# Down product of four experts: tokens moving in rows of 512, output stored by feature

## The chip, the cores and the metric

One core of one Trainium2 chip. The metric is the device time of one execution in microseconds, here the median of three runs. The core's engines are TensorE (PE in the profile; PEld is its weight load), VectorE (DVE), ScalarE (ACT), GpSimd (POOL) and SyncE (SP), whose queue issues most DMAs. SBUF is the working memory, PSUM the eight banks that TensorE writes; a bank holds 512 fp32 numbers in each of 128 partitions.

## The reference

Three layers in a row on B = 2 batches of S = 768 tokens, 1,536 tokens in all, with 384 features each.

```python
# 1: linear attention with decay, 8 heads of 48
for t in range(S):
    state = alpha[:, :, t, :, None] * state + einsum('bhd,bhe->bhde', k[:, :, t], v[:, :, t])
    y[:, :, t] = einsum('bhd,bhde->bhe', q[:, :, t], state)
# 2: RMS norm and a gated layer, 384 -> 1536 -> 384
xn = x / sqrt(mean(x * x, -1) + 1e-6) * rms_g
g = xn @ w_gate
x = (g * sigmoid(g) * (xn @ w_val)) @ w_out
# 3: four experts, 384 -> 1024 -> 384, each token with its own shares
p = domain_probs / (domain_probs.sum(-1, keepdims=True) + 1e-9)
for e in range(4):
    h = maximum(x @ w1[e], 0.0)
    out += p[:, e:e + 1] * (h @ w2[e])
```

The change touches the last line, the product with w2 and its weighting by the shares.

## The kernel before

Every fp32 product is made of three products in a reduced fp32 format: each operand is split into a high and a low part (whi and wlo, hh and hl), and high x low, high x high and low x high are added up in one PSUM bank. This is `mm3`, lines 907 to 911, so all dense matmuls bear the lines L909, L910 and L911. The three matmuls differ in the stationary operand (lhsT, loaded by a weight load) and in the moving one, whose columns stream through.

The tokens are worked in three blocks of 512. Attention goes chunk by chunk (128 tokens) and is mixed into the first two blocks of the gated layer. All work is recorded in a plan, whose list scheduler gives each operation a planned start from planned costs, due paths and buffers; the operations are then issued in that order, each on its engine's queue. There are two plans. The first holds attention and the gated layer for blocks 0 and 1, with some 35 matmuls on zeros (`idle`, L1070) that fill planned gaps of TensorE at the start. The second holds block 2 of the gated layer and the experts.

In the gated layer's down step (`outs` in `block1`) the weights are stationary and 512 hidden tokens move; its output stands by feature, three banks of 128 features. In the trace these are the rows `o<-hl,whi`, `o<-hh,whi`, `o<-hh,wlo`, 128x512. The stretch called the dense block below is block 2 of this layer and the part of block 1 without attention, from some 230 to 300 us.

The expert stage has 96 steps: expert e, block blk, and eight pieces f of 128 hidden features. An up step (`e_up`) is nine 512-wide matmuls (x2 moving) into a bank g or ph, then ScalarE's Relu (hh, L1252) and VectorE's remainder (hl, L1257). A down step (`e_down`) takes hh and hl as stationary operands, 128 tokens at a time, and moves 384 columns of w2: four token tiles of three matmuls, rows `o<-wlo,hh`, `o<-whi,hh`, `o<-whi,hl` and the same with pe. Each tile has its own bank for the eight pieces, three o banks and one pe bank. Behind the eighth piece VectorE multiplies each tile by the token's share, a scalar per partition (`pr`), and adds it to `acc` (L1291 for expert 0, L1297 after), and for the last expert SP stores the tile (L1306), 128 tokens of 384 features. On TensorE the order is up step n, then down step n - 1; only at the start stand three up steps and then two down steps.

At the end a flag decides whether `general`, a slow fallback without the splitting, runs; in this profile it doesn't.

Of the kernel before, what the change touches and what calls it, by code (L numbers as in the profile page):

```python
# [19 lines left out]
P = 128  # L20
# [208 lines left out]
def general(tc, const, af, kq, v, w64, w32, out):  # L229
# [6 lines left out]
    with ExitStack() as ctx:  # L236
# [137 lines left out]
        for e in range(E):  # L374
# [4 lines left out]
            for blk in range(4):  # L379
# [11 lines left out]
                for t in range(3):  # L391
# [16 lines left out]
                    if e == E - 1:  # L408
                        r0 = blk // 2 * S + (blk % 2 * 3 + t) * C
                        nc.sync.dma_start(out=out[r0 : r0 + C, :], in_=acc[i])  # L410
# [3 lines left out]
def body(ctx: ExitStack, tc: tile.TileContext, af, kq, v, w64, w32, rms_g, probs, out):  # L414
# [31 lines left out]
    x2_dram = dram.tile([P, KD, 512], F32, name="x2_dram")  # L446

# [609 lines left out]
    def idle(start, end):  # L1057

        gap = end - start - 0.2 - (COLD if start < 2 else 0)
        many = lambda a: a.unsqueeze(1).to_broadcast([P, 4, P])  # L1060
        row = floor[:, :512].bitcast(F32R)
        kinds = (
            (zw, zeros), (zw, row), (zw, ones[:, :1].bitcast(F32R).to_broadcast([P, 512])),
            (zw, many(zw)), (zw[:, :64], row),
            (zw.bitcast(BF16)[:, :P], floor[:, :256].bitcast(BF16)),
        )
        for n in range(max(0, round(gap / 0.22)) if start else 0):
            w, x = kinds[nfill[0] // 4 % len(kinds)]
            to = first[0]()[: w.shape[1]]
            nc.tensor.matmul(to, lhsT=w, rhs=x, start=False, stop=False)  # L1070
            nfill[0] += 1

    nfill = [0]
# [93 lines left out]
    for n in block1([(1, slice(0, 512), f) for f in range(12)]):  # L1167
# [5 lines left out]
        if n == 10:  # L1173
            plan.op("DVE", 0.5, norm_probs, r=[("x2_dram", 0)], w=["pr"])

# [89 lines left out]
    pe = {}  # L1265

    def e_down(e, blk, f):
        key = (19 + 4 * e + 2 * (f // 4), f // 2 % 2)
        hh, hl = hq.pop((e, blk, f))
        if f == 0:  # L1270
            for t in range(4):
                pe[t] = obank() if t < 3 else plan.tile(psl, [P, 512], F32, "pe", 1)
        for t in range(4):
            i = 4 * blk + t
            p, a = pe[t], acc[i]

            def go(t=t, p=p):
# [9 lines left out]
            p1 = pr[:, i, e : e + 1]  # L1287
# [99 lines left out]
```

## Time and profile before

| | us |
|---|---|
| median of 3 runs (lowest, highest) | 711.68 (711.62, 712.18) |
| the profiled execution's own time | 711.74 |
| its span, first to last instruction | 710.0 |
| TensorE busy | 697.9 |
| VectorE busy | 310.7 |
| ScalarE busy | 198.7 |

Matmuls are pipelined: a printed length of 0.39 us for a 512-wide one overlaps its neighbours, so the spacing of starts is what a matmul costs. A group's row gives count, busy time and mean length; a timeline row gives start, length, engine, line and tiles, and in brackets the idle time before it with what ended it.

### The profile page before, as it was taken

The page shows a single profiled execution, that of the slowest core. Times are in us where ns is not written, and L with a number is a line of the kernel's source. Part 1 is how long each engine was busy: PE and PEld are TensorE (multiplying, and loading weights), DVE is VectorE, ACT ScalarE, POOL GpSimd, SP SyncE. Part 2 cuts the span into 40 slices and gives each one's busy share as a digit, 9 for nine tenths or more (in the row PEclk, how much of TensorE's full clock was granted, in tenths as well). Part 3 has the DMA queues.
Part 4 walks back from the last instruction along what each step waited for, and adds up shares of the span by engine and source line. Part 5 has one row for each costly group of instructions (what it writes and reads, how often), then busy time and mean ns, then how long its engine had stood idle before and what let it go on. Part 6 is the DMA issues. An engine that isn't in the chain of part 4 may idle for free.

```text
span 710.0 us, 9804 instructions
## 1 busy us (share of the span) xinstructions
PE 697.9 (98%) x4164; PEld 610.4 (86%) x4164; DVE 310.7 (44%) x522; ACT 198.7 (28%) x406; POOL 12.9 (2%) x26
## 2 busy tenths in 40 slices
PE   8989999999999999999999999999999999999996
PEld 6889887778888888789999999999899999999996
DVE  7899999993223544432223512133312121222212
ACT  3754544543222433421113311123111111111110
POOL 1010000000000000000000000000000000000000
PEclk9999999999999999999999999999999999999999
DMA  9843554250000241310001310001000000001001
GB/s 263 262 135 109 170 192 140 78 195 2 0 1 1 90 133 46 134 45 1 1 1 44 92 42 0 1 1 44 1 1 1 0 1 1 0 1 45 23 22 47
DMA packets 13873, 42.02 MB, mean 59 GB/s; under 512 B 1856, under 2 KB 4928, under 8 KB 13824
## 3 DMA queue, kind: packets, MB, share of 16 engines
q1 hardware_dynamic: 13536, 41.32, 18.1%
q8 instruction: 33, 0.54, 0.3%
q14 instruction: 16, 0.13, 0.1%
q10 hardware_dynamic: 288, 0.03, 0.0%
HBM read 38.19 MB, written 3.15 MB: 58 GB/s over the span
## 4 chain that ended last, share of the span: by engine, by line
PE 81%; DVE 13%; DMA 3%; issue 1%; SPq 1%; ACT 0%; DVEq 0%; ACTq 0%
PE o L909 10%; PE o L911 10%; PE o L910 10%; PE g L909 9%; PE g L910 9%; PE g L911 9%; PE ph L910 5%; PE ph L911 5%; PE ph L909 5%; DMA raw<-in_w 3%; PE pe L910 2%; PE pe L909 2%; PE pe L911 2%; DVE cv L582 2%; DVE cv L574 2%; DVE wlo L517 1%
## 5 line engine op out<-in xcount | busy, mean ns | idle before, releaser
L909 PE MATMUL g<-x1l,whi 128*128 128x512 f32 (+1 forms) x384 | 146.5, 382 | 0.0
L911 PE MATMUL g<-x1h,wlo 128*128 128x512 f32 (+1 forms) x384 | 145.3, 378 | 0.0
L910 PE MATMUL g<-x1h,whi 128*128 128x512 f32 (+1 forms) x384 | 145.3, 378 | 0.0
L911 PE MATMUL o<-whi,hl 128*128 128x384 f32 x288 | 97.5, 339 | 0.0
L909 PE MATMUL o<-wlo,hh 128*128 128x384 f32 x288 | 97.3, 338 | 0.0
L910 PE MATMUL o<-whi,hh 128*128 128x384 f32 x288 | 96.9, 337 | 0.0
L1257 DVE SCALAR_TENSOR_TENSOR hl<-ph,hh 128x512 fp32r<-128x512 f32 x48 | 33.2, 691 | 128.3 <-ACT hh L1252 128.3
L1257 DVE SCALAR_TENSOR_TENSOR hl<-g,hh 128x512 fp32r<-128x512 f32 x48 | 33.0, 688 | 119.0 <-ACT hh L1252 119.0
L911 PEld LDWEIGHTS g<-x1h,wlo 128*128 128x128 f32 x384 | 72.2, 188 | 13.4
L909 PEld LDWEIGHTS g<-x1l,whi 128*128 128x128 f32 x384 | 72.2, 188 | 12.7 <-DVE s L966 0.2
L910 PEld LDWEIGHTS g<-x1h,whi 128*128 128x128 f32 x384 | 72.2, 188 | 11.6
L1252 ACT ACTIVATE hh<-g 128x512 fp32r<-128x512 f32 x48 | 28.7, 597 | 162.1 <-PE g L911 162.1
L1252 ACT ACTIVATE hh<-ph 128x512 fp32r<-128x512 f32 x48 | 28.7, 597 | 155.8 <-PE ph L911 154.5
L909 PEld LDWEIGHTS o<-wlo,hh 128*128 128x128 f32 x288 | 54.2, 188 | 4.2
L910 PEld LDWEIGHTS o<-whi,hh 128*128 128x128 f32 x288 | 54.1, 188 | 4.1
L911 PE MATMUL ph<-x1h,wlo 128*128 128x512 f32 x144 | 57.0, 396 | 0.0
L910 PE MATMUL ph<-x1h,whi 128*128 128x512 f32 x144 | 56.9, 395 | 0.0
L909 PE MATMUL ph<-x1l,whi 128*128 128x512 f32 x144 | 56.0, 389 | 0.0
L911 PEld LDWEIGHTS o<-whi,hl 128*128 128x128 f32 x288 | 54.0, 188 | 0.0
L966 DVE TENSOR_TENSOR s<-g,s 128x512 f32<-128x512 f32 (+1 forms) x40 | 25.3, 633 | 60.0 <-PE g L911 58.8
L909 PE MATMUL o<-hl,whi 128*128 128x512 f32 (+1 forms) x120 | 45.5, 379 | 1.6 <-DVE hl L976 1.6
L910 PE MATMUL o<-hh,whi 128*128 128x512 f32 (+1 forms) x120 | 44.2, 369 | 0.0
(147 smaller groups left out, 905.9 us busy)
## 6 DMA issues: line engine op xcount, KB each, us to landing
raw<-in_w SPq DMA_DIRECT2D x34, 768.0 KB, 4.4
kq<-in_kq SPq DMA_DIRECT2D x20, 224.0 KB, 3.2
out_y<-acc SPq DMA_DIRECT2D x12, 192.0 KB, 1.9
af<-in_af SPq DMA_DIRECT2D x10, 226.2 KB, 3.6
v<-in_v SPq DMA_DIRECT2D x10, 192.0 KB, 4.2
x_dram<-s SPq DMA_DIRECT2D x3, 256.0 KB, 3.5
raw<-x_dram SPq DMA_DIRECT2D x1, 768.0 KB, 4.3
wlo<-in_af SPq DMA_DIRECT2D x2, 226.2 KB, 8.9
```

The lines of the kernel that those rows point to most:

```text
L517: nc.vector.scalar_tensor_tensor(out=part(lo(), k), in0=part(t().bitcast(F32), k), scalar=gneg[:, k : k + 1], in1=part(hi().bitcast(F32), ...
L574: lambda: nc.vector.scalar_tensor_tensor(out=t(), in0=word(1), scalar=0xC0000000, in1=t(), op0=ALU.bitwise_and, op1=ALU.bitwise_or,),
L582: lambda: nc.vector.scalar_tensor_tensor(out=t(), in0=word(0), scalar=29, in1=t(), op0=ALU.logical_shift_right, op1=ALU.bitwise_or,),
L909: nc.tensor.matmul(ps_ap, lhsT=lh, rhs=rl, start=first, stop=False)
L910: nc.tensor.matmul(ps_ap, lhsT=lh, rhs=rh, start=False, stop=False)
L911: nc.tensor.matmul(ps_ap, lhsT=ll, rhs=rh, start=False, stop=last)
L966: lambda: nc.vector.tensor_mul(s()[:, :n], pv()[:, :n], s()[:, :n]), r=[pv], w=[s],
L1252: "ACT", 0.5, lambda: nc.scalar.activation(out=hh(), in_=ph(), func=AF.Relu),
L1257: lambda: nc.vector.scalar_tensor_tensor(out=hl(), in0=ph(), scalar=0.0, in1=hh().bitcast(F32), op0=ALU.max, op1=ALU.subtract,),
```

## The change

The expert's down step is turned round. The weights of w2 are stationary, and hl and hh move, 512 tokens in a row: three outputs of 128 features by 512 tokens in the three o banks, nine matmuls. The pe bank goes to ph, which has three. `acc` becomes three tiles, one per block, by feature.

A token's share now varies along the row. The shares are transposed once on TensorE in the first plan, copied by ScalarE and stored to DRAM (`p_dram`); for each expert and block SP loads 512 of them, repeated on all partitions, into a tile s. Behind the eighth piece VectorE multiplies by that tile: for expert 0 straight into `acc`, for the others in place in PSUM, followed by an addition into `acc`. For the last expert both are done in halves of 256 tokens, and SP stores each half by feature, 128 KB each. The host turns the output back.

The filling matmuls of `idle` all take the same zeros now; before they went through six kinds of operands. The fallback stores by feature as well.

```diff
+    p_dram = dram.tile([2 * NC, E, P], F32, name="p_dram")
...
         for n in range(max(0, round(gap / 0.22)) if start else 0):
-            w, x = kinds[nfill[0] // 4 % len(kinds)]
-            to = first[0]()[: w.shape[1]]
-            nc.tensor.matmul(to, lhsT=w, rhs=x, start=False, stop=False)
-            nfill[0] += 1
+            nc.tensor.matmul(first[0](), lhsT=zw, rhs=zeros, start=False, stop=False)
...
         if n == 10:
             plan.op("DVE", 0.5, norm_probs, r=[("x2_dram", 0)], w=["pr"])
+            pT = abank((2 * NC * E, P), fifo=False)
+            ps_sb = plan.tile(att, [2 * NC * E, P], F32, "x", 2)
+            plan.op(
+                "PE", 0.12,
+                lambda: nc.tensor.transpose(pT(), pr.rearrange("p i e -> p (i e)"), ident),
+                r=["pr"], w=[pT],
+            )
+            plan.op(
+                "ACT", 0.3, lambda: nc.scalar.activation(out=ps_sb(), in_=pT(), func=AF.Copy),
+                r=[pT], w=[ps_sb],
+            )
+            dma(
+                0.03,
+                lambda: nc.sync.dma_start(out=p_dram.rearrange("i e t -> (i e) t"), in_=ps_sb()),
+                r=[ps_sb], w=["p_dram"],
+            )
...
-    acc = [plan.tile(late, [P, DM], F32, f"acc{i}", 1) for i in range(2 * NC)]
+    acc = [plan.tile(late, [P, KD, 512], F32, f"acc{i}", 1) for i in range(3)]
...
-        return gbank() if nh[0] % 2 else plan.tile(psl, [P, 512], F32, "ph", 2)
+        return gbank() if nh[0] % 2 else plan.tile(psl, [P, 512], F32, "ph", 3)
...
+    def p_load(e, blk):
+
+        pb[e, blk] = t = plan.tile(hp, [P, 512], F32, "s", 3)
+        src = p_dram[4 * blk : 4 * blk + 4, e].unsqueeze(0).to_broadcast([P, 4, P])
+        dma(
+            0.26, lambda: nc.sync.dma_start(out=t().rearrange("p (i t) -> p i t", i=4), in_=src),
+            r=["p_dram"], w=[t],
+        )
...
         if f == 0:
-            for t in range(4):
-                pe[t] = obank() if t < 3 else plan.tile(psl, [P, 512], F32, "pe", 1)
-        for t in range(4):
-            i = 4 * blk + t
-            p, a = pe[t], acc[i]
-
-            def go(t=t, p=p):
-                sl = slice(t * P, (t + 1) * P)
+            for d in range(KD):
+                pe[d] = obank()
+            p_load(e, blk)
+        for d in range(KD):
+            p, a, t = pe[d], acc[blk], pb[e, blk]
+
+            def go(d=d, p=p):
                 mm3(
-                    p()[:, :DM], (hh()[:, sl], hl()[:, sl]), dn_ops(key, f, slice(0, DM)),
-                    f == 0, f == 7,
-                )
-
-            plan.op("PE", 0.522, go, r=[*units[key], hh, hl], w=[p], chain="dense")
+                    p(), dn_ops(key, f, slice(d * P, (d + 1) * P)), (hh(), hl()), f == 0, f == 7
+                )
+
+            plan.op("PE", 0.68, go, r=[*units[key], hh, hl], w=[p], chain="dense")
             if f < 7:
                 continue
...
+            last = e == E - 1
+            for c in (slice(0, 256), slice(256, 512)) if last else (slice(0, 512),):
+                n = c.stop - c.start
                 plan.op(
...
+                    "DVE", 0.07 + n / 960,
+                    lambda d=d, p=p, a=a, t=t, c=c, e=e: nc.vector.tensor_mul(
+                        a()[:, d, c] if e == 0 else p()[:, c], p()[:, c], t()[:, c]
                     ),
...
+                if e:
+                    plan.op(
+                        "DVE", 0.07 + n / 960,
+                        lambda d=d, p=p, a=a, c=c: nc.vector.tensor_add(
+                            a()[:, d, c], p()[:, c], a()[:, d, c]
+                        ),
+                        r=[p], w=[(a, d)], port=False,
+                    )
+                if last:
+                    dma(
+                        0.1,
+                        lambda d=d, a=a, c=c, blk=blk: nc.sync.dma_start(
+                            out=out[d * P : (d + 1) * P, blk * 512 + c.start : blk * 512 + c.stop],
+                            in_=a()[:, d, c],
+                        ),
+                        r=[(a, d)],
+                    )
```

TensorE's queue at one down step, the last piece of block 0 for expert 3, before (first and last of its four tiles):

```order
L909 MATMUL o_5141<-wlo_4435,hh_5304 128x384
L910 MATMUL o_5141<-whi_4433,hh_5304 128x384
L911 MATMUL o_5141<-whi_4433,hl_5309 128x384
...
L909 MATMUL pe_5157<-wlo_4435,hh_5304 128x384
L910 MATMUL pe_5157<-whi_4433,hh_5304 128x384
L911 MATMUL pe_5157<-whi_4433,hl_5309 128x384
```

And the same step now, all nine matmuls:

```order
L918 MATMUL o_4945<-hl_5095,whi_4303 128x512
L919 MATMUL o_4945<-hh_5090,whi_4303 128x512
L920 MATMUL o_4945<-hh_5090,wlo_4305 128x512
L918 MATMUL o_4952<-hl_5095,whi_4303 128x512
L919 MATMUL o_4952<-hh_5090,whi_4303 128x512
L920 MATMUL o_4952<-hh_5090,wlo_4305 128x512
L918 MATMUL o_4958<-hl_5095,whi_4303 128x512
L919 MATMUL o_4958<-hh_5090,whi_4303 128x512
L920 MATMUL o_4958<-hh_5090,wlo_4305 128x512
```

Four groups of three became three, and the first of each group reads hl, which was read by the third.

VectorE's queue behind that step, before. The first hl is the one of the last piece of block 0; the two hl behind it belong to the first two up steps of block 1:

```order
L1257 SCALAR_TENSOR_TENSOR hl_5309<-ph_5291,hh_5304 128x512
L1297 SCALAR_TENSOR_TENSOR acc0_3313<-o_5141,pr_94,acc0_3313 128x384
L1257 SCALAR_TENSOR_TENSOR hl_5339<-g_5317,hh_5330 128x512
L1297 SCALAR_TENSOR_TENSOR acc1_3323<-o_5147,pr_94,acc1_3323 128x384
L1297 SCALAR_TENSOR_TENSOR acc2_3335<-o_5153,pr_94,acc2_3335 128x384
L1297 SCALAR_TENSOR_TENSOR acc3_3337<-pe_5157,pr_94,acc3_3337 128x384
L1257 SCALAR_TENSOR_TENSOR hl_5371<-ph_5346,hh_5365 128x512
```

And now, where TENSOR_TENSOR into o is a product with the share tile s and into acc0 an addition:

```order
L1314 TENSOR_TENSOR o_4945<-o_4945,s_4553 128x256
L1271 SCALAR_TENSOR_TENSOR hl_5119<-g_5100,hh_5113 128x512
L1322 TENSOR_TENSOR acc0_3308<-o_4945,acc0_3308 128x256
L1314 TENSOR_TENSOR o_4952<-o_4952,s_4553 128x256
...
L1314 TENSOR_TENSOR o_4958<-o_4958,s_4553 128x256
L1322 TENSOR_TENSOR acc0_3308<-o_4945,acc0_3308 128x256
L1271 SCALAR_TENSOR_TENSOR hl_5148<-ph_5125,hh_5145 128x512
L1322 TENSOR_TENSOR acc0_3308<-o_4952,acc0_3308 128x256
L1322 TENSOR_TENSOR acc0_3308<-o_4958,acc0_3308 128x256
```

Five rows are left out: the third product of the first halves, two additions, and two products of the second halves. Four operations became twelve; the second addition out of o_4945, which frees the first bank, is the tenth of them, and an hl stands ahead of the last two.

VectorE's queue at the end of a block of experts 1 and 2, now (block 1 of expert 2):

```order
L1271 SCALAR_TENSOR_TENSOR hl_4728<-g_4710,hh_4723 128x512
L1314 TENSOR_TENSOR o_4555<-o_4555,s_4137 128x512
L1314 TENSOR_TENSOR o_4562<-o_4562,s_4137 128x512
L1322 TENSOR_TENSOR acc1_3501<-o_4555,acc1_3501 128x512
L1314 TENSOR_TENSOR o_4568<-o_4568,s_4137 128x512
L1322 TENSOR_TENSOR acc1_3501<-o_4562,acc1_3501 128x512
L1322 TENSOR_TENSOR acc1_3501<-o_4568,acc1_3501 128x512
L1271 SCALAR_TENSOR_TENSOR hl_4761<-ph_4734,hh_4754 128x512
```

Six operations stand between two hl, and the first bank is free after the third of them.

## Rows read from the trace of the kernel before

**Rows 1.** The page: its head, busy shares, and the chain by engine.
```profile
span 710.0 us, 9804 instructions
PE 697.9 (98%) x4164; PEld 610.4 (86%) x4164; DVE 310.7 (44%) x522; ACT 198.7 (28%) x406; POOL 12.9 (2%) x26
...
PE 81%; DVE 13%; DMA 3%; issue 1%; SPq 1%; ACT 0%; DVEq 0%; ACTq 0%
```

**Rows 2.** Windows, expert stage: length, busy us (instructions), granted clock, DMA share, GB/s.
```profile
308.00:704.00 396.00, 396.00 (x1992) 359.38 (x1990) 102.66 (x155) 67.20 (x108) 0.00 (x0) 1.00 0.05 17
```

**Rows 3.** Timeline of TensorE, dense block and expert stage.
```profile
242.42 0.39 PE L909 MATMUL o<-hl,whi 128*128 128x512 f32 x1
...
291.38 0.39 PE L909 MATMUL o<-hl,whi 128*128 128x512 f32 x1
...
302.34 0.39 PE L909 MATMUL g<-x1l,whi 128*128 128x512 f32 x1
...
308.46 0.33 PE L909 MATMUL o<-wlo,hh 128*128 128x384 f32 x1
...
310.56 0.33 PE L909 MATMUL o<-wlo,hh 128*128 128x384 f32 x1
...
312.64 0.39 PE L909 MATMUL ph<-x1l,whi 128*128 128x512 f32 x1
...
335.66 0.33 PE L909 MATMUL o<-wlo,hh 128*128 128x384 f32 x1
...
337.76 0.39 PE L909 MATMUL ph<-x1l,whi 128*128 128x512 f32 x1
...
339.84 0.33 PE L909 MATMUL o<-wlo,hh 128*128 128x384 f32 x1
...
697.81 0.39 PE L909 MATMUL ph<-x1l,whi 128*128 128x512 f32 x1
...
703.91 0.34 PE L911 MATMUL pe<-whi,hl 128*128 128x384 f32 x1
```

**Rows 4.** VectorE's groups by form: count, busy us, mean ns, idle before.
```profile
L966 DVE TENSOR_TENSOR s<-g,s 128x512 f32<-128x512 f32 x32 | 22.0, 688 | 59.9 <-PE g L911 58.8 <-issue 1.0
L976 DVE TENSOR_TENSOR hl<-s,hh 128x512 fp32r<-128x512 f32 x32 | 22.0, 686 | 10.0 <-ACT hh L971 9.8
...
L966 DVE TENSOR_TENSOR s<-g,s 128x256 f32<-128x256 f32 x8 | 3.3, 417 | 0.1
```

**Rows 5.** Timeline of VectorE: first plan, a block's end, the last operation.
```profile
36.70 0.41 DVE L966 TENSOR_TENSOR s<-g,s 128x256 f32<-128x256 f32 x1
37.03 0.95 DVE L574 SCALAR_TENSOR_TENSOR cv<-raw,cv 128x768 uint32<-128x768 uint32 x1
...
336.91 0.68 DVE L1257 SCALAR_TENSOR_TENSOR hl<-g,hh 128x512 fp32r<-128x512 f32 x1
337.51 1.13 DVE L1291 TENSOR_SCALAR acc<-o,pr 128x384 f32<-128x384 f32 x2
...
340.67 0.69 DVE L1257 SCALAR_TENSOR_TENSOR hl<-ph,hh 128x512 fp32r<-128x512 f32 x1 [1.50 <-ACT hh L1252]
...
704.31 0.61 DVE L1297 SCALAR_TENSOR_TENSOR acc<-pe,pr,acc 128x384 f32<-128x384 f32 x1
```

**Rows 6.** The output's stores: issue time in ns, first and last issue, landing.
```profile
L1306 SPq DMA_DIRECT2D out_y<-acc x12: 332/333/1005, 638.5 to 705.5; - x12
...
DMA to landing us min/median/max: 1.9/1.9/3.1
```

**Rows 7.** TensorE's group of transposes in the first plan.
```profile
L854 PE MATMUL att<-ident,x 128*128 128x128 f32 x36 | 6.4, 286 | 0.0
```

**Rows 8.** The page's DMA issues: the stores of x2, KB each, us to landing.
```profile
x_dram<-s SPq DMA_DIRECT2D x3, 256.0 KB, 3.5
```

**Rows 9.** Timeline of TensorE: eight of the filling matmuls.
```profile
7.33 1.08 PE L1070 MATMUL o<-zw 128*128 128x512 f32 x4
8.25 1.09 PE L1070 MATMUL o<-floor,zw 128*64 128x512 f32 x4
```

More of the change, by code (lines that the diff above doesn't have):

```diff
@@ L408, in general @@
                     if e == E - 1:
-                        r0 = blk // 2 * S + (blk % 2 * 3 + t) * C
-                        nc.sync.dma_start(out=out[r0 : r0 + C, :], in_=acc[i])
+                        p = ps.tile([P, half], F32, name="up", bufs=4)
+                        for d in range(KD):
+                            sl = slice(d * P, (d + 1) * P)
+                            nc.tensor.transpose(p[:, sl], acc[i][:, sl], ident)
+                        y = sb.tile([P, half], F32, name="m")
+                        nc.scalar.activation(out=y, in_=p, func=AF.Copy)
+                        nc.sync.dma_start(
+                            out=out[:, i * C : (i + 1) * C].rearrange("(d p) t -> p d t", p=P),
+                            in_=y.rearrange("p (d t) -> p d t", d=KD),
+                        )
 @with_exitstack
@@ L1263, in e_up @@
         hq[e, blk, f] = (hh, hl)
-    pe = {}
+    pe, pb = {}, {}
+    def p_load(e, blk):
[5 more added lines that the diff above has]
+        )
     def e_down(e, blk, f):
@@ L1282, in go @@
+            p_load(e, blk)
+        for d in range(KD):
+            p, a, t = pe[d], acc[blk], pb[e, blk]
+            def go(d=d, p=p):
+                mm3(
+                    p(), dn_ops(key, f, slice(d * P, (d + 1) * P)), (hh(), hl()), f == 0, f == 7
                 )
-            plan.op("PE", 0.522, go, r=[*units[key], hh, hl], w=[p], chain="dense")
+            plan.op("PE", 0.68, go, r=[*units[key], hh, hl], w=[p], chain="dense")
             if f < 7:
                 continue
-            p1 = pr[:, i, e : e + 1]
@@ L1288, in e_down @@
-            if e == 0:
+            last = e == E - 1
+            for c in (slice(0, 256), slice(256, 512)) if last else (slice(0, 512),):
+                n = c.stop - c.start
                 plan.op(
-                    "DVE", 0.47,
-                    lambda p=p, a=a, p1=p1: nc.vector.tensor_scalar_mul(a(), p()[:, :DM], p1),
-                    r=[p], w=[a],
-                )
-            else:
-                plan.op(
-                    "DVE", 0.53,
-                    lambda p=p, a=a, p1=p1: nc.vector.scalar_tensor_tensor(
-                        out=a(), in0=p()[:, :DM], scalar=p1, in1=a(), op0=ALU.mult, op1=ALU.add
-                    ),
-                    r=[p], w=[a],
-                )
@@ new lines, in e_down @@
+                    r=[t, p], w=[(a, d) if e == 0 else p], port=False,
+                )
+                if e:
[12 more added lines that the diff above has]
+                            in_=a()[:, d, c],
+                        ),
+                        r=[(a, d)],
+                    )
@@ L1381 @@
     ]
-    o = nc.dram_tensor("out_y", (NT, DM), F32, kind="ExternalOutput").ap()
+    o = nc.dram_tensor("out_y", (DM, NT), F32, kind="ExternalOutput").ap()
     with tile.TileContext(nc) as tc:
@@ L1385 @@
     r = run_bass_kernel_spmd(nc, [{f"in_{k}": a for k, a in arrays.items()}], core_ids=[0])
-    return r.results[0]["out_y"]
+    y = r.results[0]["out_y"].reshape(DM, NC, B, C)
+    return np.ascontiguousarray(y.transpose(2, 1, 3, 0)).reshape(NT, DM)
```

14 lines of the change are left out of this document (removed).

## The prediction

> **What bounds the kernel now.** First the page's busy shares and its chain of waits [rows 1]: TensorE is busy for 98% of the span and holds 81% of the chain. The stretches of the second plan sharpen this [rows 2]: from 308 to 704 us TensorE is busy all 396 us at a granted clock of 1.00, its upper level of 2.4 GHz, while VectorE works 102.7 us. So in the expert stage time is matmul count times matmul spacing, and any other engine matters only where it makes TensorE wait.
>
> The spacing comes from TensorE in order of time, by starts, since the printed lengths overlap [rows 3]. Four facts:
> - Dense block, 512-wide matmuls throughout: from 242.42 to 291.38 us eight periods of 27 matmuls, 48.96 / 216 = 0.2267 us each, so 2.04 us for nine.
> - The first three up steps of the experts stand behind one another, 302.34 to 308.46: 6.12 / 3 = 2.04 us. The expert stage can run at the same rate.
> - Then come two down steps in a row. The second, 310.56 to 312.64, takes 2.08 us for its twelve 384-wide matmuls, 0.1733 us each; the first takes 2.10.
> - In the steady alternation a down step takes 2.10 us (335.66 to 337.76) and an up step 2.08 (337.76 to 339.84). From 312.64 to 697.81 stand 92 rounds of one up and one down: 4.187 us each, though the undisturbed steps would make 2.04 + 2.08 = 4.12.
>
> So a round pays twice: 0.04 us because twelve 384-wide matmuls cost more than nine 512-wide ones, and 0.067 us for alternating the two widths, which shows in both steps. The dense block, which also alternates up and down but in one width, pays neither.
>
> **The change part by part.** The sum is made against the profiled execution: 711.74 us, a span of 710.0 and 1.74 around it; the median of the runs is 711.68, so the two agree.
>
> *Matmuls.* Each of the 96 down steps goes from twelve matmuls of 384 columns to nine of 512. Weights now stand still and tokens move, which is exactly the dense block's down step; the three outputs of 128 features replace four of 128 tokens. Afterwards 192 steps of one width follow each other: 192 x 2.04 = 391.7 us. Before, the same work ran from 302.34 to the end of the last matmul's slot, 703.91 + 0.17 = 704.08, or 401.7. Gain: 10.1 us. The first matmul of a step now needs hl, where it was the third; hl is ready 0.83 + 0.69 us after the up step ends [rows 3 to 5], and a down step of 2.04 us lies in between, so this costs nothing.
>
> *Bank waits at block ends.* Shares can no longer be a per-partition scalar. From the second expert on, each 512-wide output takes a product in place in PSUM and an addition; with three o banks and no pe bank, the next block's first down step waits for the additions. VectorE's 512-wide operation with a PSUM input lasts 0.69 us and the 256-wide one 0.42 [rows 4], but the next one starts after 0.60 (336.91 to 337.51) and 0.33 (36.70 to 37.03) [rows 5]. Let time zero be the start of a block's last down step; the next one wants its banks at 4.08, 4.76 and 5.44 us. Experts two and three (six ends): hl at 0.83, then product, product, addition, product, addition, addition every 0.60, so the additions end at 3.32, 4.52 and 5.12. All are in time, the second by 0.24 less a wake-up, which I take as the 0.06 us between the modelled end of the last matmul (703.91 + 0.34) and VectorE's start at 704.31 [rows 3, 5]. Cost taken: 0.05 each, 0.3 in all; at 0.69 spacing it would be 0.32 each, 1.9 in all.
> Expert four (two ends) does worse. Its operations are halved, and the order puts all first halves ahead of the second ones, one hl in front and another in between: the first bank's second addition is the tenth of twelve and ends at 4.91, the other two banks' at 5.93 and 6.26, behind the next step's hl, which can't start before that up step's end plus 0.83. TensorE stands 0.9 us, and 0.3 more before the second output: 1.25 each, 2.5 in all. The first expert has three products only, and its banks are free in time.
>
> *The end.* Before, 704.08 to 710.0 is 5.9 us after the last matmul's slot. Afterwards twelve half-width operations follow the start of the last down step: the first output is ready at 0.9 (two matmul starts, 0.45, then 0.39 and 0.06), eleven spacings of 0.33, one addition right behind its own product (0.1 more), and the last one's full length: 0.9 + 11 x 0.33 + 0.1 + 0.42 = 5.1 us, or 3.05 after the slot. From the last issue of an output to the span's end stand 710.0 - 705.5 = 4.5 us, with landings between 1.9 and 3.1 us [rows 1, 6]. Two thirds of the bytes in each transfer and the first three transfers long gone, I take 3.9: 3.05 + 0.06 + 3.9 = 7.0, a loss of 1.1 (0.5 if the last lands in 1.9, 1.7 if nothing shortens).
>
> *Small parts.* One transpose of the shares on TensorE: its nearest row is 0.286 us, start to end [rows 7]; beside others it is 0.1 (0 to 0.3). Its ScalarE copy and the store of 24 KB wait on SP just ahead of the load of fit, which waits there anyway. The twelve loads of repeated shares are 256 KB each; such a transfer landed 3.5 us after issue [rows 8], and each is issued at least one block, 8 rounds or some 33 us, before it is read. That also covers SP's order, where weight loads now stand behind share loads that wait for a buffer. The filling matmuls keep their number and only their operands change; four zeros took 1.08 us, four of another kind 1.09 [rows 9]: nothing. The fallback isn't run.
>
> Sum: -10.1 + 0.3 + 2.5 + 1.1 + 0.1 = -6.1, so 705.7 us.
>
> *A rule against it.* The page "TensorE: Matmul & The Clock Gate" of the Trainium skill (section Back-to-back issue gap) has columns over clock plus 2.5 ns. An estimate by that page of the Trainium skill is 288 fewer matmuls x 2.5 ns = 0.7 us of gain, and a sum of +3.3: 715.0. The trace disagrees: 0.2267 and 0.1733 us are 13 ns above columns over 2.4 GHz. The Trainium skill's page "VectorE: DVE Perf Modes" (section The DRAIN you can't avoid) says that the next operation starts only when the pipe is empty, so that op count is what to save; the 0.60 spacing of 0.69 us operations contradicts it here; the third rival below is priced by the full lengths of the rows.
>
> **The rivals.**
> 1. *The alternation cost belongs to the expert stage, not to the two widths.* Then only the 0.04 us per down step goes: 96 x 0.04 = 3.8, and the sum is +0.2: 711.9. If every step takes the 2.08 us of today's up steps, the gain is some 2.5 and the time 713.2. For it: the up steps are already 512 wide and still take 2.08. Against it: three of them took 2.04 before the first down step, and the dense block never leaves 2.04.
> 2. *Slower: the in-place products.* No VectorE operation of the trace writes PSUM. If reading and writing there take turns, a product's spacing grows by its streaming time, 0.53 at 512 (twice the 0.27 between the two sizes' spacings): 1.13 and 0.60. The same chains then end so late that TensorE stands 1.4 us at six ends and 2.75 at two, and the end loses 2.7: -10.1 + 8.5 + 5.5 + 2.7 + 0.1 = +6.7, 718.4. It decides from a mean stall of 1.1 us at the eight ends. Against it: the 512-wide operation that reads PSUM (688 ns) is no longer than the one that stays in SBUF (686) [rows 4].
> 3. *VectorE spacing is the full length* (0.69 and 0.42). Six ends 0.32, two 2.2, the end 1.9: -10.1 + 1.9 + 4.4 + 1.9 + 0.1 = -1.8, 709.9.
> 4. *Slower: columns alone count.* A step keeps 12 x 384 = 9 x 512 = 4,608 columns; with no gain there, +4.0: 715.7. The 2.08 against 2.04 us speaks against it.
>
> **How the numbers follow.** Forecast 0.80, first rival 0.08, second 0.05, third 0.05, fourth 0.02. The forecast's own range is 703.2 (no stall in expert four, a short end) to 708.5 (0.32 at six ends, a long end) and holds nine tenths of it; with the third rival and the space between, 703.2 to 710.5 holds 8 in 10. A measurement here can tell 0.2%, 1.4 us, from no change. Faster by more: 0.80 + most of the third and a little of the first, 0.84; within: half of the first, 0.04; slower: 0.12.
>
> **What would show it.** In the expert stage the starts of 512-wide matmuls 0.227 us apart and rounds of 4.08 us; 0.231 would mean the first rival. At the two block ends of expert four TensorE idle 0.9 us before an o matmul and 0.3 before another, released by VectorE's additions; at the six earlier ends nothing or under 0.1. The 512-wide products 0.69 us long and 0.60 apart; 1.2 would mean the second rival. The last addition 3 us after the last matmul's slot. The forecast is wrong if the rounds stay above 4.12 us or if idle time of TensorE in the expert stage exceeds 6 us.

## The result and the profile after

| | us | ratio to the kernel before (95% interval) |
|---|---|---|
| the kernel before, median of 6 (lowest, highest) | 711.65 (711.44, 712.77) | |
| the changed kernel, median of 6 | 705.79 (705.01, 706.30) | 0.9913 (0.9900, 0.9926) |
| its profiled execution; span | 706.3; 704.6 | |

The forecast was 705.7. The page of the changed kernel answers to [rows 1]: head and busy shares.

```profile
span 704.6 us, 9312 instructions
...
PE 688.9 (98%) x3877; PEld 570.7 (81%) x3877; DVE 323.9 (46%) x555; ACT 199.2 (28%) x407; POOL 13.0 (2%) x26
```

There are 287 matmuls fewer (288 out of the down steps, one transpose in), and TensorE is still busy 98% of a shorter span. The window over the expert stage answers to [rows 2]; columns as there.

```profile
308.00:697.00 389.00, 387.20 (x1705) 319.23 (x1703) 113.56 (x181) 67.28 (x108) 0.00 (x0) 1.00 0.07 23
```

Before, TensorE was busy for all of that stretch; now 1.8 us are open. The clock is the same upper level. TensorE in order of time answers to [rows 3]: start, length, engine, line, matmul, and in brackets the idle time with what ended it. (mm3 now has the lines L918 to L920.)

```profile
302.44 0.39 PE L918 MATMUL g<-x1l,whi 128*128 128x512 f32 x1
...
337.12 0.39 PE L918 MATMUL ph<-x1l,whi 128*128 128x512 f32 x1
...
339.16 0.39 PE L918 MATMUL o<-hl,whi 128*128 128x512 f32 x1
...
341.20 0.39 PE L918 MATMUL g<-x1l,whi 128*128 128x512 f32 x1
...
632.92 0.39 PE L920 MATMUL ph<-x1h,wlo 128*128 128x512 f32 x1
634.10 0.47 PE L918 MATMUL o<-hl,whi 128*128 128x512 f32 x1 [0.79 <-DVE acc L1322]
634.40 0.40 PE L919 MATMUL o<-hh,whi 128*128 128x512 f32 x1
634.63 0.40 PE L920 MATMUL o<-hh,wlo 128*128 128x512 f32 x1
635.14 0.47 PE L918 MATMUL o<-hl,whi 128*128 128x512 f32 x1
635.45 0.39 PE L919 MATMUL o<-hh,whi 128*128 128x512 f32 x1
...
696.96 0.39 PE L920 MATMUL o<-hh,wlo 128*128 128x512 f32 x1
```

The reader is to see two things. An up step (337.12 to 339.16) and a down step (339.16 to 341.20) both take 2.04 us: a round is 4.08, where it was 4.187. And TensorE stands at 634.10, where VectorE's addition releases a bank: 1.18 us from start to start in place of 0.227, then 0.51 at the second output (634.63 to 635.14). The first matmul behind each pause takes 0.30 to the next start, 0.08 more than usual. That makes 0.95 + 0.08 + 0.28 + 0.08 = 1.4 us; the same pattern stands at 668.17, and nowhere else in the stage.

VectorE's groups by form answer to [rows 4]:

```profile
L1314 DVE TENSOR_TENSOR o<-o,s 128x512 f32<-128x512 f32 x18 | 11.9, 690 | 0.0
L1322 DVE TENSOR_TENSOR acc<-o,acc 128x512 f32<-128x512 f32 x18 | 11.8, 681 | 0.0
...
L1322 DVE TENSOR_TENSOR acc<-o,acc 128x256 f32<-128x256 f32 x18 | 6.9, 416 | 0.0
...
L1314 DVE TENSOR_TENSOR o<-o,s 128x256 f32<-128x256 f32 x18 | 6.8, 425 | 8.3 <-PE o L920 8.3
```

Its timeline answers to [rows 5]: the end of a block of expert three, one of expert four, and the end of the kernel. A row with x2 or x3 joins operations that stand behind one another.

```profile
532.40 1.29 DVE L1314 TENSOR_TENSOR o<-o,s 128x512 f32<-128x512 f32 x2
533.60 0.68 DVE L1322 TENSOR_TENSOR acc<-o,acc 128x512 f32<-128x512 f32 x1
534.20 0.69 DVE L1314 TENSOR_TENSOR o<-o,s 128x512 f32<-128x512 f32 x1
534.79 1.28 DVE L1322 TENSOR_TENSOR acc<-o,acc 128x512 f32<-128x512 f32 x2
...
632.54 1.09 DVE L1314 TENSOR_TENSOR o<-o,s 128x256 f32<-128x256 f32 x3
633.53 0.42 DVE L1322 TENSOR_TENSOR acc<-o,acc 128x256 f32<-128x256 f32 x1
633.97 0.69 DVE L1271 SCALAR_TENSOR_TENSOR hl<-ph,hh 128x512 fp32r<-128x512 f32 x1
634.58 0.75 DVE L1322 TENSOR_TENSOR acc<-o,acc 128x256 f32<-128x256 f32 x2
...
699.15 1.08 DVE L1322 TENSOR_TENSOR acc<-o,acc 128x256 f32<-128x256 f32 x3
```

Products in place in PSUM last 0.69 and 0.42 us like their neighbours, and the next operation starts after 0.60 (532.40 to 533.60 for two) and 0.33 (632.54 to 633.53 for three). The addition that frees the first bank is the one that ends at 633.95, and TensorE starts at 634.10; the last two additions stand behind hl, and the second bank comes free at about 635.0. The last operation ends at 699.15 + 1.08 = 700.23, 3.05 us after the last matmul's slot (696.96 + 0.227 = 697.185).

The stores of output answer to [rows 6]: issue time in ns, first and last issue, landing.

```profile
L1330 SPq DMA_DIRECT2D out_y<-acc x18: 332/342/422, 631.3 to 700.5; - x18
...
DMA to landing us min/median/max: 1.7/1.7/2.6
```

From the last slot to the span's end are 704.565 - 697.185 = 7.4 us; before it was 5.9. The last store is issued at 700.49, 0.26 us after VectorE's end: with its neighbours it stands in SP's queue, where an issue takes 0.33 to 0.40 us and the additions come every 0.33. The twelve loads of shares are on the page's list of DMA issues (KB, us to landing), and TensorE never waits for one:

```profile
s<-p_dram SPq DMA_DIRECT2D x12, 256.0 KB, 3.5
```

The balance of the two profiled executions: the expert stage, from its first matmul to the end of the last slot, went from 401.74 to 394.74 us (-7.0, waits included), the end from 5.92 to 7.38 (+1.46), and the stage began 0.1 later. Together -5.4, the difference of the spans 710.0 and 704.6.

### The profile page after: what moved, and what is told of

Read it like the earlier page. It is cut to its first block, busy times and chain, and to the rows that moved or that the text cites. A ratio compares the mean times of both kernels' runs of the same rounds, so it can differ in the third digit from the quotient of the medians.

```text
span 704.6 us, 9312 instructions
## 1 busy us (share of the span) xinstructions
PE 688.9 (98%) x3877; PEld 570.7 (81%) x3877; DVE 323.9 (46%) x555; ACT 199.2 (28%) x407; POOL 13.0 (2%) x26
## 5 line engine op out<-in xcount | busy, mean ns | idle before, releaser
L918 PE MATMUL o<-hl,whi 128*128 128x512 f32 (+1 forms) x408 | 158.0, 387 | 3.2 <-DVE acc L1322 1.6
L920 PE MATMUL o<-hh,wlo 128*128 128x512 f32 (+1 forms) x408 | 156.3, 383 | 0.0
L919 PE MATMUL o<-hh,whi 128*128 128x512 f32 (+1 forms) x408 | 156.2, 383 | 0.0
L918 PE MATMUL g<-x1l,whi 128*128 128x512 f32 (+1 forms) x384 | 146.5, 381 | 0.0
L920 PE MATMUL g<-x1h,wlo 128*128 128x512 f32 (+1 forms) x384 | 144.4, 376 | 0.0
L918 PEld LDWEIGHTS o<-hl,whi 128*128 128x128 f32 x408 | 76.6, 188 | 20.7 <-PE ph L920 2.4
L920 PEld LDWEIGHTS o<-hh,wlo 128*128 128x128 f32 x408 | 76.6, 188 | 15.2
L919 PEld LDWEIGHTS o<-hh,whi 128*128 128x128 f32 x408 | 76.7, 188 | 14.4
L918 PEld LDWEIGHTS g<-x1l,whi 128*128 128x128 f32 x384 | 72.2, 188 | 14.0 <-DVE s L975 0.2
L920 PEld LDWEIGHTS g<-x1h,wlo 128*128 128x128 f32 x384 | 72.2, 188 | 13.3
L918 PE MATMUL ph<-x1l,whi 128*128 128x512 f32 x144 | 56.0, 389 | 0.0
L920 PE MATMUL ph<-x1h,wlo 128*128 128x512 f32 x144 | 56.0, 389 | 0.0
L493 DVE TENSOR_TENSOR wlo<-raw,whi 128x768 fp32r<-128x768 f32 x32 | 30.6, 956 | 20.4 <-ACT whi L488 20.1
L967 ACT ACTIVATE s<-g 128x512 f32<-128x512 f32 (+1 forms) x40 | 22.1, 552 | 53.0 <-PE g L920 52.6
```

Source lines behind the costliest of these rows:

```text
L493: lambda: nc.vector.tensor_tensor(out=lo(), in0=src_ap(), in1=hi().bitcast(F32), op=ALU.subtract),
L918: nc.tensor.matmul(ps_ap, lhsT=lh, rhs=rl, start=first, stop=False)
L919: nc.tensor.matmul(ps_ap, lhsT=lh, rhs=rh, start=False, stop=False)
L920: nc.tensor.matmul(ps_ap, lhsT=ll, rhs=rh, start=False, stop=last)
L967: lambda: nc.scalar.activation(out=s()[:, :n], in_=pg()[:, :n], func=AF.Silu),
```

## The experiments

The theory after this: rounds became shorter because one width of moving operand is left, the two waits come from the order of the halves on VectorE, and the end is VectorE's queue of halves. Ten runs test it. The first four ask where the 2.08 us of an up step came from. Where a time is compared with the kernel before, that ran on the same chip in the same comparison. The first three runs had one execution each, the profiled one; step lengths below are distances of matmul starts.

**A narrower moving operand in the new orientation.** In the changed kernel the down pieces behind the first of each block move 384 tokens of the 512:

```diff
+                w = 384 if f else 512
...
-                    p(), dn_ops(...), (hh(), hl()), f == 0, f == 7
+                    p()[:, :w], dn_ops(...), (hh()[:, :w], hl()[:, :w]), f == 0, f == 7
```

> The changed kernel, but for pieces f = 1 to 7 the down step moves only the first 384 of the block's 512 tokens (the products of the others are left out for these pieces). Roles, order and count of the matmuls stay; only the width of the down step differs from that of the up step. Theory (two widths in alternation cost): the steps behind a change of width are disturbed again, as in the kernel before: up steps 2.08 us instead of 2.04, down steps 9 x 0.173 + 0.026 = 1.59 us; time about 671. Rival (it was the hidden tokens as stationary operand, not the width): up steps stay 2.04, down steps 1.56; time about 666.

Measured: 676.5 us. TensorE's timeline, an up step, a down step, and the next up step's start:

```profile
451.80 0.39 PE L918 MATMUL g<-x1l,whi 128*128 128x512 f32 x1
...
453.88 0.33 PE L918 MATMUL o<-hl,whi 128*128 128x384 f32 x1
...
455.47 0.39 PE L918 MATMUL ph<-x1l,whi 128*128 128x512 f32 x1
```

The up step is back at 2.08 us, and the down step takes 1.585 where nine times 0.1733 would be 1.56. The nine distances of the up step are 229 to 236 ns with one of 224, those of the down step 170, 175, 178, 185, 176, 181, 174, 173, 173: the disturbance of the kernel before, with weights stationary and tokens moving. So it belongs to two widths that alternate, not to the orientation. The time is 5.5 us higher than expected; two reasons make 4.5 of them. A shorter down step leaves VectorE less time: TensorE now also waits 0.31 us (a distance of 535 ns) at six block ends beside the two of expert four, with the 0.08 behind each pause 6 x 0.39 + 2 x 1.54 = 5.4 us where the changed kernel has 2.8. And the stage began 1.9 us later than in the changed kernel's profile (last section).

**448 tokens.** The same edit with 448.

> As the run before it, with 448 tokens moving in pieces 1 to 7. A 448-wide matmul should start every 0.200 us, longer than the 0.188 us that a weight load takes; a 384-wide one starts every 0.173 us, shorter than that load. Theory A (any two widths disturb each other): up steps above 2.04 us, towards 2.08. Theory B (the disturbance comes from weight loads longer than the spacing of the matmuls that cover them): up steps 2.04 and down steps 9 x 0.200 = 1.80 us, nothing disturbed.

Measured: 691.9 us. The timeline, a down step, an up step, the next start, and the first and last matmul of the run's last down step:

```profile
451.83 0.36 PE L918 MATMUL o<-hl,whi 128*128 128x448 f32 x1
...
453.66 0.39 PE L918 MATMUL ph<-x1l,whi 128*128 128x512 f32 x1
...
455.73 0.36 PE L918 MATMUL o<-hl,whi 128*128 128x448 f32 x1
...
680.66 0.36 PE L918 MATMUL o<-hl,whi 128*128 128x448 f32 x1
...
682.29 0.36 PE L920 MATMUL o<-hh,wlo 128*128 128x448 f32 x1
```

Down 1.824, up 2.069 us. The up step is 0.029 above 2.04, and its first six distances are 229 to 235 ns, the last three 226 and 227. The down step is 0.024 above the 1.80 that theory B put down, but that looks like the width's own rate and not like a disturbance: the last down step of the run stands behind another of the same width, and its eight distances (from 680.66 on) are still 199 to 207 ns, 202.75 on average, where 1.824 / 9 is 202.7. So matmuls of 448 columns start 16 ns above columns over 2.4 GHz, where 384 and 512 start 13.3 ns above; why, no run here shows. Both second widths that were tried disturb the up step behind them, the nearer one less. That a weight load (0.188 us in the records) must be longer than the spacing of the matmuls is refuted: here all distances of the down step are 199 to 207 ns.

**The old orientation in one width.** In the kernel before, the down step moves 512 columns instead of 384 (of w2 and of what stands beside it, so the sums are other ones):

```diff
+                o = f % 2 * 256
...
-                    p()[:, :DM], (hh()[:, sl], hl()[:, sl]), dn_ops(key, f, slice(0, DM)),
+                    p(), (hh()[:, sl], hl()[:, sl]), tuple(w()[:, o : o + 512] for w in units[key]),
```

> The kernel before, with hidden tokens stationary and twelve matmuls per down step, but each moves 512 columns of w2's tile instead of 384 (128 of them belong to the neighbouring piece, so the output is not the reference's). Theory (two widths cost): with one width the up step falls from 2.08 to 2.04 us, the down step is 12 x 0.2267 = 2.72; rounds of 4.76 us, time about 767. Rival (the stationary operand's role costs): up steps stay at 2.08 us and down steps are above 2.72; rounds of 4.80 or more, time 771 or more.

Measured: 765.9 us, within 0.2% of what was expected. An up step, a down step of twelve, the next start:

```profile
452.12 0.39 PE L909 MATMUL g<-x1l,whi 128*128 128x512 f32 x1
...
454.16 0.39 PE L909 MATMUL o<-wlo,hh 128*128 128x512 f32 x1
...
456.88 0.39 PE L909 MATMUL ph<-x1l,whi 128*128 128x512 f32 x1
```

2.04 and 2.72 us, which is twelve times 0.2267: nothing is lost to which operand stands still. With the two runs above this settles that which operand stands still is itself worth nothing. What the turn gives is the one width, and nine matmuls in place of twelve.

**Half as many changes of width.** In the kernel before, two up steps and then two down steps:

```diff
-        if n > 1:
-            if n == 2:
-                e_down(*es[0])
-            e_down(*es[n - 1])
+        if n > 1 and n % 2:
+            e_down(*es[n - 3])
+            e_down(*es[n - 2])
```

(and a fourth pair of hh and hl tiles, and the last two down steps at the end).

> The kernel before with another order of TensorE's steps: two up steps, then two down steps, so half as many changes of width; nothing else differs but a fourth pair of hidden tiles. Theory: the 0.067 us belong to a change of width, so half of 96 rounds save them: -3.2 us, about 708.5; the second step of each pair undisturbed (up 2.04, down 2.08). Rival (each step of the expert stage is slow by itself): no gain, 711.7.

Measured: 706.95 us against 711.12, ratio 0.9941 (0.9922, 0.9960). The starts of a first up step, a second one, and the down step behind it:

```profile
454.59 0.39 PE L909 MATMUL g<-x1l,whi 128*128 128x512 f32 x1
...
456.67 0.39 PE L909 MATMUL ph<-x1l,whi 128*128 128x512 f32 x1
...
458.71 0.33 PE L909 MATMUL o<-wlo,hh 128*128 128x384 f32 x1
```

The first up step takes 2.08, the second 2.04; of the twenty-four 384-wide matmuls behind them only the first six are disturbed, 26 ns in all. The stage lasts 398.4 us from its first matmul start to its last, against 401.57 in the kernel before: 3.1 us less, as expected. (The medians differ by 4.2. What exceeds 3.1 doesn't lie in the stage: in the profiles it began 1.3 us earlier here, and the end was 1.4 us shorter.) The changed kernel's stage is 7.0 us shorter, 10.0 without its waits; 3.1 of these were thus to be had by the order of the steps alone, with half of the changes of width left, and without any new wait.

**Halves only where they are needed.** In the changed kernel, halves in the last block of expert four alone:

```diff
-            for c in (slice(0, 256), slice(256, 512)) if last else (slice(0, 512),):
+            for c in (slice(0, 256), slice(256, 512)) if last and blk == 2 else (slice(0, 512),):
```

> The changed kernel with VectorE's products and additions in halves only in the last block of expert four; the other two blocks of expert four get whole 512-wide operations, as experts two and three have them. My theory: TensorE waits at the two block ends of expert four (2.8 us in the changed kernel) because all first halves are ordered ahead of the second ones, so that a bank comes free only with the last operations. Then these two ends behave like the six earlier ones (0.05 us each) and the time falls by about 2.7 us, from 705.8 to about 703.1. Rival: expert four's ends are late for another reason that the halves don't set (its stores of output, issued there, or the loads); then gaps of 0.5 us and more stay at 634 and 668 us, and the time by less than 1 us different.

Measured: 703.0 us against 710.51, ratio 0.9889 (0.9869, 0.9909). Where the wait stood, at the end of expert four's first block, TensorE's timeline now reads:

```profile
632.19 0.39 PE L920 MATMUL ph<-x1h,wlo 128*128 128x512 f32 x1
632.42 0.39 PE L918 MATMUL o<-hl,whi 128*128 128x512 f32 x1
```

0.227 us and no pause; no distance of starts in the stage is above 0.255. From its first to its last matmul start the stage takes 391.93 us (301.58 to 693.51), 2.6 less than the 394.52 of the changed kernel. The halves, in the order in which they stood, were the cause of both waits; the rival falls. All eight ends now show the same 0.06 us, 0.04 in one step and 0.02 in the next.

**The last outputs one by one.** Besides, halves only for the last output of the last block, and that block's last two pieces in the order of outputs:

```diff
-    e_down(*es[-1])
+    for d in range(KD):
+        e_down(*es[94], [d])
+        e_down(*es[95], [d])
```

(and in the loop before it the last down steps move back accordingly).

> As the run without halves, and besides the last block's last two down pieces are done output by output (piece 6 and piece 7 of the first output, then of the second, then of the third), so that VectorE can finish the first two outputs while TensorE still works; VectorE takes product and addition of an output one behind the other, and only the third output is in halves. My theory: the end of the changed kernel (7.4 us after the last matmul's slot) holds 3.05 us of VectorE's twelve operations behind one another; with one output left, its four half operations end about 1.6 us after the slot, so another 1.4 us go: about 701.7. Rival: the end is set by the issue and landing of the stores, whatever VectorE does; then the time equals that of the run without halves, about 703.1.

Measured: 700.52 us against 710.51, ratio 0.9852 (0.9831, 0.9873). VectorE's last three operations:

```profile
694.54 0.42 DVE L1322 TENSOR_TENSOR acc<-o,acc 128x256 f32<-128x256 f32 x1
695.00 0.43 DVE L1314 TENSOR_TENSOR o<-o,s 128x256 f32<-128x256 f32 x1
695.46 0.42 DVE L1322 TENSOR_TENSOR acc<-o,acc 128x256 f32<-128x256 f32 x1
```

The expectation missed two sizes. VectorE ends at 695.89, 2.0 us after the last slot and not 1.6: each operation now stands right behind one on the same output and starts after that has ended, so they start 0.46 apart and not 0.33. And what follows VectorE's end became shorter as well, from 4.3 to 3.2 us. Four stores are left at the end instead of six; the last is issued 0.02 us after VectorE's end and lands in 1.7 us, where it was 0.26 and 2.6. So the end was partly VectorE's queue (1.0 us) and partly the stores behind it (1.1 us). That the last one was slow for the number of stores is a reading: with six of them it took 2.5 to 2.7 us in seven profiles, with four 1.7 and 1.8 in two, but nothing varied their number alone.

**Products to SBUF.** In the changed kernel, halves as they are, each product goes to a tile q and the addition reads that:

```diff
+            q = plan.tile(late, [P, 512], F32, "q", 3) if e else None
...
-                        a()[:, d, c] if e == 0 else p()[:, c], p()[:, c], t()[:, c]
+                        a()[:, d, c] if e == 0 else q()[:, c], p()[:, c], t()[:, c]
...
-                            a()[:, d, c], p()[:, c], a()[:, d, c]
+                            a()[:, d, c], q()[:, c], a()[:, d, c]
```

> The changed kernel, but each product is written to a tile in SBUF instead of in place to its PSUM bank; halves as they are. My theory: the in-place write costs VectorE nothing (products stay at 0.69 us for 512 columns and 0.42 for 256, spacing 0.60 and 0.33), but it holds a bank until its addition has been done; with the product in SBUF a bank is free after the product, some operations earlier, so that the gaps at the two ends of expert four shrink. Their last bank's second product then is the operation that TensorE waits for, where it was the second addition; with up to 1.4 us less at each end the time is between 703.1 and 704.5, the end unchanged. Rival: an in-place write to PSUM is slower than one to SBUF; then the products' spacing falls below 0.60 and 0.33 us and the end of the kernel (3.05 us from the last slot to VectorE's last operation) shortens by more than 0.3 us.

Measured: 702.44 us against 710.51, ratio 0.9879 (0.9858, 0.9901), a little under the range that was expected. VectorE's groups of products:

```profile
L1315 DVE TENSOR_TENSOR q<-o,s 128x512 f32<-128x512 f32 x18 | 11.3, 681 | 0.0
...
L1315 DVE TENSOR_TENSOR q<-o,s 128x256 f32<-128x256 f32 x18 | 6.4, 417 | 1.4 <-PE o L920 1.4
```

681 and 417 ns against 690 and 425 in place: the write to PSUM costs 8 to 9 ns in an operation's length and nothing in the spacing, and VectorE's end moves by 0.09 us only. The stage takes 391.46 us, with no wait left at all, though the halves are there. The expectation still had the second product of the last bank as something to wait for; in fact the order changed too: all six products stand first, and are done before TensorE wants the first bank. The 0.06 us at the other ends are gone as well. This run thus changed two things at once, when a bank comes free and the order of the operations; what each is worth alone it doesn't show.

**The old filling matmuls.** The changed kernel with the six kinds of operands for `idle`, as before.

> The changed kernel with the six kinds of filling matmuls of the kernel before in the first plan. My theory: the kind of operand doesn't matter; the time is that of the changed kernel, 705.8 with 0.7 either way, and the expert stage starts within 0.2 us of 302.45. Rival: uniform fillers shift the clock or the order in the first plan; then the start of the expert stage moves by over 0.5 us.

Measured: 705.0 us against 710.51, ratio 0.9918 (0.9898, 0.9938). The ratio is that of the changed kernel, and the stage takes 394.58 us. But the stage began at 301.03, 1.4 us earlier than in the changed kernel's profile, so the rival's mark was met. It proves nothing: other variants, with the fillers of the changed kernel, began between 301.58 and 304.34. See the last section.

**Both, and the changed kernel again.** Products to SBUF, outputs one by one, and for the last output the two half products ahead of the two half additions:

```diff
+            for c in cs:
...
+            for c in cs:
...
```

(the first loop has the products of an output's halves, the second the additions and stores).

> The run with the last outputs one by one, and besides every product goes to a tile in SBUF, and the last output's two half products stand ahead of its two half additions, so that no addition waits for the product just ahead of it. My theory: without a bank held through the addition the expert stage needs 391.5 us from its first to its last matmul start, where the run with the last outputs one by one needed 391.88; and the four half operations at the end start 0.33 us apart instead of 0.47, so VectorE ends 1.85 us after the last matmul's start instead of 2.24. Together 0.8 us less: 699.7 beside that run's 700.5. Rival: the order of products and additions doesn't matter at the end, because the next operation waits for the transfer or the bank; then 2.24 us stay, and the stage alone gives 0.4.

Measured: 700.15 us against 711.73, ratio 0.9832 (0.9815, 0.9850), the lowest here. TensorE's first and last matmul of the stage:

```profile
302.79 0.39 PE L918 MATMUL g<-x1l,whi 128*128 128x512 f32 x1
...
694.25 0.39 PE L920 MATMUL o<-hh,wlo 128*128 128x512 f32 x1
```

and VectorE's last operations:

```profile
694.67 0.76 DVE L1316 TENSOR_TENSOR q<-o,s 128x256 f32<-128x256 f32 x2
695.34 0.75 DVE L1326 TENSOR_TENSOR acc<-q,acc 128x256 f32<-128x256 f32 x2
```

391.46 us for the stage, with all 191 distances between step starts from 2.039 to 2.045 us, and VectorE's end 1.85 us after the last matmul's start: both as expected. In the traces that is 0.7 us (391.46 and 5.18 to the end) less than the run with outputs one by one (391.88 and 5.43); the two ratios' intervals overlap, so the times alone don't separate them.

> The changed kernel once more, unedited, on the chip of the run above. My theory: it takes 5.5 us less than the kernel before (as in the two comparisons so far, 5.9 with its own fillers and 5.5 with the old ones), and 6 us more than the run above; what differs from execution to execution lies in the first 55 us, before the dense block. Rival: the expert stage or the end varies from execution to execution; then the 394.5 us between the first and last matmul start of the stage, or the 7.6 us behind them, move by over 0.5 us.

Measured: 706.49 us against 711.73, ratio 0.9922 (0.9906, 0.9938); 5.2 us less than before and 6.3 more than the run above. Stage 394.68 and 7.53 behind it, beside 394.52 and 7.61 in the first profile: both repeat to 0.2 us.

## Why the prediction was right

- **Matmuls, -10.1.** Without the two waits and the next point's 0.23 the stage is 394.74 - 2.8 - 0.23 = 391.7 us, as forecast. The reading that carried it was that three up steps in a row took 2.04 before the first down step and 2.08 ever after [rows 3], so the extra belongs to alternating. (Between an up step and its own down step lie two steps, 4.08 us, and not the one of 2.04 that the prediction counted; hl is in time either way.) The first rival, that it belongs to the stage, is refuted by 2.04 for both steps, and by the run with 384 tokens, where it came back. The fourth, that columns alone count, falls with the same rounds. The prediction's rule from the page "TensorE: Matmul & The Clock Gate" of the Trainium skill, section Back-to-back issue gap, falls too: 2.5 ns above columns over clock would have left 715.0, and here it is 13.3 ns, for 512 and for 384 columns (0.2267 and 0.1733 us). But that section of the Trainium skill gives the formula for an isolated matmul; where every matmul has its weight load, as here (3,877 of each), it says that both set the spacing, and its figure for 512 columns is some 131 ns. The trace doesn't show that either.
- **Six ends, +0.3.** Measured 0.23: four ends cost 0.05 to 0.06 and two nothing; in the repeat all six cost 0.06. As the run with products in SBUF shows, even that comes with banks that are freed just in time. That the size fits is luck. The prediction had 0.24 us of slack less 0.06 at the second bank and took its 0.05 without a working. It counted to the matmul, but the weight load in front of it (PEld) waits for the bank too, and that one is wanted 0.22 us earlier. At the end of expert three's block whose VectorE rows stand above:

```profile
535.27 0.19 PEld L920 LDWEIGHTS o<-hh,wlo 128*128 128x128 f32 x1
535.53 0.19 PEld L918 LDWEIGHTS o<-hl,whi 128*128 128x128 f32 x1
...
535.50 0.40 PE L920 MATMUL o<-hh,wlo 128*128 128x512 f32 x1
535.73 0.40 PE L918 MATMUL o<-hl,whi 128*128 128x512 f32 x1
535.97 0.39 PE L919 MATMUL o<-hh,whi 128*128 128x512 f32 x1
```

(Weight loads above, TensorE's matmuls below.) The second addition ends at 535.475 (534.79 + 0.68), and 0.05 us later, at 535.53, the second output's weight load starts, 0.03 behind the start of the matmul ahead of it (535.50), where 0.003 is usual. So it is at all six ends: the slack is gone by 0.03 us. Where it costs anything, the matmuls behind it are disturbed up to the middle of the next step (last section), and that makes most of the 0.06.
- **Expert four, +2.5.** Measured 2.8. The place, the order and the releaser were as forecast (0.95 before the first output for 0.9, 0.28 before the second for 0.3); missing were the 0.08 us that the first matmul after each pause costs. Its weight load starts only 0.03 us ahead of it (the load at 634.07, the matmul at 634.10), in the unbroken stream 0.22.
- **The end, +1.1.** Measured +1.46: VectorE's end at 3.05 us after the slot exactly as forecast, but then 4.3 us and not 3.9 + 0.06. Some 0.2 of that is SP's queue, which issues the last store 0.26 us after VectorE's end; the rest lies behind the issue. Stores of 128 KB land in 1.7 us, but the last of six issued within 4 us takes 2.6. The comparison flatters the change: in the profile of before one store took 1.0 us to issue [rows 6], and in the run with pairs, whose end has the same code, there were 4.7 us from the last matmul start to the span's end, not 6.1. Beside 4.7 the changed kernel's 7.6 would be a loss of 2.9. The kernel before has one profile only, so how often its end is the long one stays open.
- **In-place products.** The second rival priced reading and writing PSUM as taking turns; a spacing of 0.60 and 0.33 refutes it. The third rival, full-length spacing, falls with the same rows. The Trainium skill's page "Perfetto Trace Analysis" (section Optimizing Scalar/DVE Operations) says why a length can exceed a spacing: part of it, the acknowledgement of the write, lies beside the next operation. The trace agrees for independent operations (0.60 for 0.69). So the prediction goes too far where it has the 0.60 contradict the Trainium skill's page "VectorE: DVE Perf Modes": the section The DRAIN you can't avoid adds that an operation that isn't held (made to wait for all before it) starts earlier, and the 0.60 agrees with that. The trace doesn't agree with the "Perfetto Trace Analysis" page's higher overhead on PSUM than in SBUF (Trainium skill, the same section): three additions wholly in SBUF, in the last variant, span 1.89 us and so stand 0.60 apart as well.
- **Small parts.** Loads of shares landed in 3.5 us (median) as forecast and nobody waits for them; transpose and fillers can't be told from what an execution's start varies by.

In sum the forecast has -6.1 and the two profiles -5.4: 0.3 more in the waits and 0.4 more at the end; the rest of the steps came out to 0.1. The medians differ by 5.9. So the mechanism held part by part, but that the median lies within 0.1 us of 705.7 is luck: in the two profiles the sum is 0.7 off, and the executions differ among themselves by more than that.

## What to carry to other kernels

Where TensorE is full, look at the distances of matmul starts, not at busy shares: of the 10.0 us some 6.3 were the alternation of widths (0.067 a round) and 3.8 the twelve narrower matmuls of a step (0.04 each). Grouping steps of one width gave 3.1 without turning an operand. A bank that is released by the second of two operations makes a full TensorE wait even where VectorE is idle most of the time, so write the first result to SBUF, count a bank's deadline to the weight load in front of the matmul, and use halves only where the end of the kernel depends on them. At the end, hand over outputs one by one: both the queue of operations and the crowd of stores become shorter.

## What the runs showed of the hardware that was not expected

- A change of moving width disturbs the matmuls behind it, and not only the first: from 384 to 512 columns the nine behind it take 40 ns more in all, from 512 to 384 the first six 26 ns (0.1733 each being undisturbed); between 448 and 512 it is 29 ns in the up step. A second step of the same width is undisturbed. But a change of width isn't the only thing that sets this off: behind the short wait at 535.73 of the changed kernel, where all matmuls are 512 wide, nine distances are 229, 234, 235, 225, 230, 236, 229, 232 and 231 ns, and in an up step of the kernel before (492.67) they are 229, 235, 235, 224, 231, 236, 229, 232 and 230. What in the engine does it, no run here shows.
- A matmul that starts after a pause of 0.08 us or more takes 0.08 us more until the next one starts, at every such pause in the stage of five profiles.
- A weight load waits for the bank of its matmul: at the six block ends of experts two and three the second output's load starts 0.05 us after the addition that frees the bank, in three profiles. In the unbroken stream it starts 0.22 us ahead of its matmul.
- The first 55 us vary. Between the profiles of the changed kernel and of its variants the start of the expert stage lies between 301.03 and 304.34 us; compared matmul by matmul, the shift is there by 55 us and then stays within 0.2 us. In this stretch the loads of the first plan are in flight; which of them sets it was not followed. Gains of 1 us are thus better read between two instructions of the trace than from the time of a few executions.
